# Attention with hashed masks, then a gated feed-forward: reordered turns, a later weight conversion and fewer transfers by ScalarE

## The chip, the cores and the metric

The kernel runs on one core of a Trainium2 chip. The time is that of the device, from start to end of the program, in microseconds (us); the median of 3 runs is 885.48 us (884.9 to 885.76). The profile is of one execution, with a span of 883.4 us from its first to its last instruction. The core's engines are TensorE (PE; its weight loads are the row PEld), VectorE (DVE), ScalarE (ACT), GpSimd (POOL) and SyncE (SP), which here only issues transfers (DMA).

## The reference

```python
batch, n_heads, seq, head_dim = (4, 8, 768, 64)          # q, k, v; proj is 64 x 6
q_bucket, k_bucket = ...    # 6 bits each: the signs of q @ proj and k @ proj
mask = q_bucket[:, :, :, None] == k_bucket[:, :, None, :]
scores = np.where(mask, np.matmul(q, k.transpose(0, 1, 3, 2)) / 8, -1e9)
attn = softmax(scores)                                     # over the keys, 1e-9 added to the sum
x = (attn @ v).transpose(0, 2, 1, 3).reshape(3072, 512)
h = x @ w_in                                               # 512 x 2048, given in float64
g = h * (1.0 / (1.0 + np.exp(-1.702 * h)))
return (g @ w_out).astype(np.float32)                      # 2048 x 512, given in float64
```

## The kernel before

Attention goes through 16 pairs of heads, n = 0 to 15, each in two halves of the queries, c = 0 and 1. (Pair 0 is cut finer, into four groups.) A group's body is given below. The instructions of TensorE, VectorE, ScalarE and GpSimd run in the order in which the code has them; those of SyncE are ordered by a scheduler. The scores come transposed (keys on the partitions): a product of small integer "feature" rows (`kf`, `qf`, from the hash bits) brings the mask into the same bank, and one exponential per tile of 128 keys unloads it.

```python
def featured(n):                        # hash bits -> feature rows, spread by 8 small transfers
    nc.vector.tensor_scalar(f, dots.pop(n), above[:, 0:1], weight[:, 0:1], ...)          # L413
    for c in range(2):
        for i, x in enumerate("kq"):
            queue = nc.scalar if (n, x) == (1, "q") else nc.sync
            for j in range(2):
                queue.dma_start(out=feats[n % 2][x][...], in_=f[...])                    # L420

def scores(n, c, kts):
    for kt in kts:
        ps = sps.tile(...)                                # three of these
        ... 2 products kf x qf and 2 products kT x qT into ps                            # L432
        nc.scalar.activation(es[c][:, kt, :, 0:HS], ps[...], Act.Exp, ...)               # L433

def values(n, c, kts):
    if 0 in kts:
        avs[n, c] = aps.tile([P, HS + 1], F32, tag="av", name="av")                      # one bank
    ... 12 products of v and e into av                                                   # L456

def unload(n, c): ...                   # ScalarE: av -> xT                              # L467, L468
def total(n): ...                       # TensorE: the sums of the exponentials, dn, in the one bank "m"
def invert(n):
    nc.vector.transpose(rt, accs.pop(n))                                                 # L484
    nc.vector.reciprocal(r, ...)        # 5 of them                                      # L486, L490
    nc.vector.transpose(rs, r)                                                           # L492

def begin(n):
    if n - 1 < len(in_chunks) - LATE:                     # 14 chunks of w_in, pairs 1 to 14
        conv[n] = convert(cv, *in_chunks[n - 1], nc.sync if n > 1 else nc.scalar)
        step(n)                                           # the load

for g in range(len(groups) + 2):                          # one group per half of a pair
    scores(n, c, kts)
    add_low(n, c)                       # GpSimd: acc0 = sum of the lower three e          L440, L441
    if hashes: featured(hashes.pop())
    add_high(*prev[:2])                 # VectorE: acc = sum of the upper three and acc0   L446, L448
    for x in turned:                    # "kq" in the first half of a pair
        turn(n + 1, x)                  # VectorE: kT, qT of the next pair                 L391
        measure(n + 1, x)               # ScalarE: their largest size                      L398
    while norms: norm(norms.pop(0))     # VectorE: xT *= rs                                L497
    if totals and totals[0][0] == g:
        norms.append(totals.pop(0)[1])
        total(norms[-1])
        invert(norms[-1])
    values(*prev)
    unload(*prev[:2])
    if "q" in turned: hashed(n + 1)     # TensorE, into "m"; then fetch q, k of pair n + 2
    step(n, 3)                          # three steps of the conversion
    if c == 0 and n > last - len(x_sums): x_sums[n - last - 1]()   # VectorE, pairs 12 to 15
    if c == 1: begin(n + 1)
    if g == len(groups) - 1: guard(0)   # VectorE: largest of all sizes
    if g == len(groups):
        guard(1)                        # TensorE turns it into "m" (row), VectorE reduces
        ...                             # GpSimd: sums of the first weights (s_in)
        next(ff)                        # the feed-forward begins
```

The conversion of a chunk of `w_in` from float64 is six operations of VectorE (L178, L182, L186 in the first half of a pair, L193, L195, L198 in the second) and one of ScalarE (L190, a square, issued with L186).

The feed-forward does both its products with seven instead of eight block products (Strassen-Winograd), twice nested in the second. Its last part, for the output, goes by steps `o` of seven products each; `after(0)` to `after(3)` are called within a step, between its unloading operations:

```python
def turned(c, i, j, q0, q1):            # VectorE: quarters of a block transposed into y[j]  L791
def written(sb, j, halves, queues):
    for b in halves:
        for a in range(4):
            queues[a % len(queues)].dma_start(out=dst, in_=ys[j][...])                   # L799

def after(at):
    if at == 0:
        while pending: pending.pop(0)()
    ...                                 # VectorE: sums of the next step's operands (t1, b12, t2, t4)
    if final and at == 2:
        for q in (0, 1, 3): turned(m, 1, 0, q, q + 1)
        written(sb, 0, (1,), loader + [nc.scalar])
    if final and at == 3:
        turned(m, 1, 0, 2, 3)
        written(sb, 0, (0,), loader + [nc.scalar])
...
elif o in (2, 3):
    pending.append(lambda a=ms[o], j=int(o == 3): turned(a, 0, j, 0, 4))
    if o == 3:
        pending.append(lambda sb=sb: written(sb, 1, (0, 1), loader))
```

Of the kernel before, what the change touches and what calls it, by code (L numbers as in the profile page):

```python
# [8 lines left out]
F32 = mybir.dt.float32  # L9
# [10 lines left out]
P = 128  # L20
# [18 lines left out]
def kernel(  # L39
# [17 lines left out]
    nc = tc.nc  # L57

    loader = [nc.sync]
# [223 lines left out]
    def attention(ff):  # L283
# [4 lines left out]
        with actx:  # L288
# [122 lines left out]
            def featured(n):  # L411
                f = wk.tile([P, HS], BF16, tag="f", name="f", bufs=1)
                nc.vector.tensor_scalar(f, dots.pop(n), above[:, 0:1], weight[:, 0:1], op0=Alu.is_gt, op1=Alu.mult)  # L413
                for c in range(2):
                    for i, x in enumerate("kq"):

                        queue = nc.scalar if (n, x) == (1, "q") else nc.sync
                        for j in range(2):
                            r0 = D * i + 32 * c + 2 * NB * j
                            queue.dma_start(out=feats[n % 2][x][D * j : D * j + 2 * NB, c * HS : (c + 1) * HS],  # L420
                                            in_=f[r0 : r0 + 2 * NB, :])
# [27 lines left out]

            def values(n, c, kts):  # L450
                if 0 in kts:
                    avs[n, c] = aps.tile([P, HS + 1], F32, tag="av", name="av")
                av, vt = avs[n, c], vts[n]
                for t in kts:
                    for j in range(2):
                        nc.tensor.matmul(av[D * j : D * (j + 1), :], vt[:, t, j, :], es[c][:, t, j, :],  # L456
                                         start=(t == 0), stop=(t == T - 1))
# [21 lines left out]
            def invert(n):  # L479


                dn = accs.pop(n)
                rt = st.tile([P, HS // 32, 32], F32, tag="rt", name="rt", bufs=1)
                nc.vector.transpose(rt.rearrange("p s i -> p (s i)"), dn)  # L484
                r = st.tile([P, 2, HS // 32], F32, tag="r", name="r")
                nc.vector.reciprocal(r, rt[:, :, 0].unsqueeze(1).to_broadcast([P, 2, HS // 32]))  # L486
                for r0 in range(0, P, 32):
                    c = r0 // 32 % 2
                    r1 = r0 + 32 - 64 * c
                    nc.vector.reciprocal(r[r1 : r1 + 32, c], rt[r0 : r0 + 32, :, 0])  # L490
                rs = accs[n] = st.tile([P, S], F32, tag="rs", name="rs", bufs=1)
                nc.vector.transpose(rs.rearrange("p (s i) -> p s i", i=32),  # L492
                                    r.rearrange("p c s -> p (c s)").unsqueeze(2).to_broadcast([P, S // 32, 32]))
# [13 lines left out]
                    next(conv.get(n, iter(())), None)  # L507

            def begin(n):
                if n - 1 < len(in_chunks) - LATE:  # L510

                    conv[n] = convert(cv, *in_chunks[n - 1], nc.sync if n > 1 else nc.scalar)
                    step(n)


# [16 lines left out]
            for g in range(len(groups) + 2):  # L532
                n, c, kts = groups[g] if g < len(groups) else (last + 1, 0, ())
                prev = groups[g - 1] if 1 <= g <= len(groups) else None
                if kts:
                    scores(n, c, kts)
                    if g == 0:
                        rest()
                    if kts[0] == 0:
                        add_low(n, c)  # L540


                if hashes:
                    featured(hashes.pop())
                ended = prev and prev[2][-1] == T - 1
                if ended:
                    add_high(*prev[:2])
                    if prev[1] == 1:
                        totals.append((g + (g == len(groups)), prev[0]))

                turned = ("", "k", "q", "")[g] if n == 0 else "kq" if c == 0 and n < last else ""
                for x in turned:
                    turn(n + 1, x)
                    measure(n + 1, x)
                while norms:
                    norm(norms.pop(0))
                if totals and totals[0][0] == g:
                    norms.append(totals.pop(0)[1])
                    total(norms[-1])
                    invert(norms[-1])  # L560
                if prev:
                    values(*prev)
                if ended:
                    unload(*prev[:2])
                if "q" in turned:
                    hashed(n + 1)
                    if n:
# [102 lines left out]
    def feed_forward(tag, late=()):  # L670
# [9 lines left out]
        with ExitStack() as fctx:  # L680
# [110 lines left out]
                    nc.vector.transpose(y, c[:, q].rearrange("p (b t) -> p b t", t=32))  # L791

            def written(sb, j, halves, queues):
                for b in halves:
                    blocks = slice(b * (TH // 32), (b + 1) * (TH // 32))
                    for a in range(4):
                        t0 = (2 * sb + j) * XT + b * TH
                        dst = out[t0 : t0 + TH, a * P : (a + 1) * P].rearrange("(b t) d -> t b d", t=32)
                        queues[a % len(queues)].dma_start(out=dst, in_=ys[j][32 * a : 32 * (a + 1), blocks, :])  # L799

            def product_of_halves(n, acc, after):

# [98 lines left out]
            for n, (sb, o) in enumerate(steps_out):  # L901
# [11 lines left out]
                def after(at):  # L913
# [15 lines left out]
                if o == 3:  # L929
# [6 lines left out]
                if o == 5:  # L936
# [13 lines left out]
    def whole(steps):  # L950
        for _ in steps:
            pass
# [46 lines left out]
```

## Time and profile before

| what | number |
|---|---|
| median time | 885.48 us |
| span of the profile | 883.4 us |
| TensorE clock granted, mean | 0.997 |
| score products L432, exponentials L433 | 155.1 us and 150.9 us busy |
| value products L456 | 131.8 us busy |
| bytes moved by DMA | 132.01 MB, mean 149 GB/s |

The page gives for each engine the time in which it was busy. Such a time says little by itself where several engines are nearly full; it has to be held against the waits, which name for every engine the instruction that it waited for, and the chain of waits, which follows the end of the program back to what released each step. A row of a transfer on SyncE or ScalarE is the time of its issue. Line numbers such as L432 are those of the kernel before.

### The profile page before, as it was taken

The page shows a single profiled execution, that of the slowest core. Times are in us where ns is not written, and L with a number is a line of the kernel's source. Part 1 is how long each engine was busy: PE and PEld are TensorE (multiplying, and loading weights), DVE is VectorE, ACT ScalarE, POOL GpSimd, SP SyncE. Part 2 cuts the span into 40 slices and gives each one's busy share as a digit, 9 for nine tenths or more (in the row PEclk, how much of TensorE's full clock was granted, in tenths as well). Part 3 has the DMA queues.
Part 4 walks back from the last instruction along what each step waited for, and adds up shares of the span by engine and source line. Part 5 has one row for each costly group of instructions (what it writes and reads, how often), then busy time and mean ns, then how long its engine had stood idle before and what let it go on. Part 6 is the DMA issues. An engine that isn't in the chain of part 4 may idle for free.

```text
span 883.4 us, 11926 instructions
## 1 busy us (share of the span) xinstructions
PE 866.9 (98%) x4077; PEld 498.4 (56%) x4077; DVE 724.9 (82%) x1020; ACT 313.3 (35%) x519; POOL 319.9 (36%) x275
## 2 busy tenths in 40 slices
PE   9899999999999999999999999999999999999995
PEld 5344444444444444444444444444888888888884
DVE  4599999999999956777777887888898977897785
ACT  5666677667667732223232223322000000000000
POOL 4244334333433363775433444559932000000000
PEclk9999999999999999999999999999999999999998
DMA  4755454566544103555456545575844665467524
GB/s 103 115 90 83 84 104 81 94 101 102 85 83 83 46 1 131 201 195 190 164 193 212 200 166 200 185 253 172 306 142 186 210 220 200 165 207 239 191 96 99
DMA packets 169477, 132.01 MB, mean 149 GB/s; under 512 B 123936, under 2 KB 138432, under 8 KB 164032
## 3 DMA queue, kind: packets, MB, share of 16 engines
q1 hardware_dynamic: 167712, 129.69, 51.7%
q10 hardware_dynamic: 1696, 1.48, 0.6%
q8 instruction: 34, 0.56, 0.3%
q14 instruction: 35, 0.29, 0.1%
HBM read 79.69 MB, written 50.33 MB: 147 GB/s over the span
## 4 chain that ended last, share of the span: by engine, by line
PE 96%; DVE 1%; DMA 1%; ACTq 0%; issue 0%; POOL 0%; ACT 0%; SPq 0%; POOLq 0%; DVEq 0%
PE product L699 33%; PE product L812 28%; PE ps L432 17%; PE av L456 14%; PE dn L477 1%; PE hash L408 1%; DMA q<-in_q_dram 1%; PE tp L366 1%; ACTq L420 0%; DVE xT L816 0%; PE hash L373 0%; DVE y L791 0%; SPq L328 0%; DMA qf<-f 0%; DVE rs L492 0%
## 5 line engine op out<-in xcount | busy, mean ns | idle before, releaser
L433 ACT ACTIVATE e<-ps 128x768 f32<-128x768 f32 x192 | 150.9, 811 | 18.4 <-PE ps L432 12.4
L432 PE MATMUL ps<-qT,kT 64*128 64x384 f32 x768 | 155.1, 482 | 0.0
L699 PE MATMUL product<-xT,w_in_sb 128*128 128x512 f32 x288 | 135.4, 592 | 0.0
L456 PE MATMUL av<-e,v 128*64 128x385 f32 x768 | 131.8, 490 | 0.9 <-ACT xT L468 0.9
L440 POOL TENSOR_TENSOR acc<-e 128x768 f32<-128x768 f32 x32 | 58.6, 1832 | 193.3 <-DVE acc L448 166.3
L707 ACT ACTIVATE c<-c 128x512 f32<-128x512 f32 x72 | 45.3, 630 | 186.3 <-issue 78.6
L456 PEld LDWEIGHTS av<-e,v 128*64 128x64 f32 x768 | 52.1, 136 | 77.6 <-issue 76.1
L699 PEld LDWEIGHTS product<-xT,w_in_sb 128*128 128x128 f32 x288 | 54.6, 190 | 68.5 <-issue 63.3
L699 PE MATMUL product<-t_x,s_in 128*128 128x512 f32 x192 | 90.2, 592 | 0.0
L432 PEld LDWEIGHTS ps<-qT,kT 64*128 64x128 f32 x768 | 68.2, 188 | 34.9 <-issue 34.8
L219 POOL TENSOR_TENSOR v<-c,u 128x512 f32<-128x512 f32 x24 | 34.1, 1423 | 127.7 <-ACT c L707 127.7
L818 ACT COPY u<-product 128x256 f32<-128x256 f32 x21 | 7.8, 372 | 167.7 <-PE product L812 125.5
L432 PE MATMUL ps<-qf,kf 64*128 64x384 bf16 x384 | 63.1, 324 | 2.9 <-ACT e L433 2.8
L699 PEld LDWEIGHTS product<-t_x,s_in 128*128 128x128 f32 x192 | 36.5, 190 | 45.9 <-issue 43.8
L441 POOL TENSOR_TENSOR acc<-acc,e 128x768 f32<-128x768 f32 x32 | 59.0, 1845 | 2.5
L699 PE MATMUL product<-xT,s_in 128*128 128x512 f32 x96 | 45.1, 592 | 0.0
L699 PE MATMUL product<-t_x,w_in_sb 128*128 128x512 f32 x96 | 45.1, 592 | 0.0
L432 PEld LDWEIGHTS <-kf 64*128 64x128 bf16 x384 | 19.1, 94 | 44.9 <-issue 23.4
L446 DVE SCALAR_TENSOR_TENSOR acc<-e 128x768 f32<-128x768 f32 x32 | 30.5, 954 | 7.7 <-ACT e L433 7.7
L467 ACT COPY vs<-av 128x1 f32<-128x1 f32 x32 | 5.1, 159 | 87.2 <-PE av L456 87.2
L812 PE MATMUL product<-raw_g,xT 128*128 128x256 f32 x152 | 35.1, 379 | 0.0
L448 DVE TENSOR_TENSOR acc<-acc,e 128x768 f32<-128x768 f32 x32 | 32.0, 999 | 3.3
(207 smaller groups left out, 1544.3 us busy)
## 6 DMA issues: line engine op xcount, KB each, us to landing
raw_g<-g_dram SPq DMA_DIRECT2D x22, 1024.0 KB
s_in<-g_dram SPq DMA_DIRECT2D x20, 1024.0 KB
g_dram<-c SPq DMA_DIRECT2D x72, 256.0 KB
g_dram<-t SPq DMA_DIRECT2D x48, 256.0 KB
raw<-in_moe_w_out_dram SPq DMA_DIRECT2D x16, 512.0 KB
raw<-in_moe_w_in_dram SPq DMA_DIRECT2D x15, 512.0 KB
v<-in_v_dram SPq DMA_DIRECT2D x32, 192.0 KB
g_dram<-u SPq DMA_DIRECT2D x24, 256.0 KB
```

The source lines that it names most:

```text
L219: return [lambda: eng.tensor_tensor(t1, b12, b11, op=Alu.subtract), lambda: eng.tensor_tensor(b12, b22, b12, op=Alu.subtract), lambda: eng ...
L366: nc.tensor.matmul(tp[D * j : D * (j + 1), i * P : (i + 1) * P], x[name][:, j, c * GT + i, :], ident, start=True, stop=True)
L432: nc.tensor.matmul(ps[:, j, 0:HS], a[hs, keys], m[hs, cols], start=not last, stop=last)
L433: nc.scalar.activation(es[c][:, kt, :, 0:HS], ps[:, :, 0:HS], Act.Exp, scale=1.0 / D**0.5)
L440: nc.gpsimd.tensor_tensor(acc, es[c][:, 0, :, 0:HS], es[c][:, 1, :, 0:HS], op=Alu.add)
L441: nc.gpsimd.tensor_tensor(acc, acc, es[c][:, 2, :, 0:HS], op=Alu.add)
L446: nc.vector.scalar_tensor_tensor(acc, e[0], T * TINY, e[1], op0=Alu.add, op1=Alu.add)
L448: nc.vector.tensor_tensor(acc, acc, x, op=Alu.add)
L456: nc.tensor.matmul(av[D * j : D * (j + 1), :], vt[:, t, j, :], es[c][:, t, j, :], start=(t == 0), stop=(t == T - 1))
L699: nc.tensor.matmul(ps, wq[LEFT[i]][:, kc, :], xq[RIGHT[i]][:, kc, :], start=(kc == 0), stop=(kc == K2 - 1))
L707: nc.scalar.activation(c, c, Act.Gelu_apprx_sigmoid)
L812: nc.tensor.matmul(ps, wq[LEFT[i]][:, c, :], gq[RIGHT[i]][:, c, :], start=(c == 0), stop=(c == F4 - 1))
```

## The change

It has six parts: pair 1's feature rows for the queries are issued by ScalarE for one half of the queries only; a chunk of `w_in` is converted one pair later, and its first load is issued by SyncE; the sums are turned (the first operation of `invert`) between the turn of the keys and that of the queries; the last values take the bank "m", so as not to wait for the unloading of the ones before, and the guard's two parts come two groups earlier; the keys of pair 2 are fetched a group earlier in the code; and at the end the last two products are turned back quarter by quarter within their steps, and the output is written by fewer transfers on two queues.

```diff
-                        queue = nc.scalar if (n, x) == (1, "q") else nc.sync
+                        queue = nc.scalar if (n, x, c) == (1, "q", 0) else nc.sync
...
-                    avs[n, c] = aps.tile([P, HS + 1], F32, tag="av", name="av")
+                    pool, tag = (mps, "m") if (n, c) == (last, 1) else (aps, "av")
+                    avs[n, c] = pool.tile([P, HS + 1], F32, tag=tag, name="av")
...
-                nc.vector.transpose(rt.rearrange("p s i -> p (s i)"), dn)
+                nc.vector.transpose(rt.rearrange("p s i -> p (s i)"), accs.pop(n))
+                yield
...
-                if n - 1 < len(in_chunks) - LATE:
-                    conv[n] = convert(cv, *in_chunks[n - 1], nc.sync if n > 1 else nc.scalar)
+                if 0 <= n - 2 < len(in_chunks) - LATE:
+                    conv[n] = convert(cv, *in_chunks[n - 2])
                     step(n)
...
-                for x in turned:
+                inverted = iter(())
+                for x in turned[:1]:
                     turn(n + 1, x)
                     measure(n + 1, x)
...
                     total(norms[-1])
-                    invert(norms[-1])
+                    inverted = invert(norms[-1])
+                    next(inverted)
+                for x in turned[1:]:
+                    turn(n + 1, x)
+                    measure(n + 1, x)
+                whole(inverted)
...
-                    for x in "kq":
+                    for x in "kq" if n else "q":
                         if n + 2 <= last:
                             fetch(n + 2, x)
                     fetch_v(n + 1)
+                elif turned:
+                    fetch(n + 2, turned)
...
-                if g == len(groups) - 1:
-                    guard(0)
+                if g in (len(groups) - 3, len(groups) - 2):
+                    guard(g - len(groups) + 3)
                 if g == len(groups):
-                    guard(1)
...
             def written(sb, j, halves, queues):
-                for b in halves:
-                    blocks = slice(b * (TH // 32), (b + 1) * (TH // 32))
-                    for a in range(4):
-                        ...
-                        queues[a % len(queues)].dma_start(out=dst, in_=ys[j][32 * a : 32 * (a + 1), blocks, :])
+                first, last = halves[0] * TH, (halves[-1] + 1) * TH
+                for a in range(4):
+                    ...
+                    queues[a % len(queues)].dma_start(out=dst, in_=ys[j][32 * a : 32 * (a + 1), first // 32 : last // 32, :])
...
-                    if final and at == 2:
-                        for q in (0, 1, 3):
-                            turned(m, 1, 0, q, q + 1)
-                        written(sb, 0, (1,), loader + [nc.scalar])
-                    if final and at == 3:
-                        turned(m, 1, 0, 2, 3)
-                        written(sb, 0, (0,), loader + [nc.scalar])
+                    if n + 2 >= len(steps_out):
+                        for q in ((0,), (), (1, 3), (2,))[at]:
+                            turned(m, int(final), int(not final), q, q + 1)
+                    if final and at >= 2:
+                        written(sb, 0, (3 - at,), loader + [nc.scalar])
+                    if n + 2 == len(steps_out) and at == 3:
+                        written(sb, 1, (0, 1), loader + [nc.scalar])
...
-                elif o in (2, 3):
+                elif o in (2, 3) and n + 2 < len(steps_out):
```

More of the change, by code (lines that the diff above doesn't have):

```diff
@@ L479, in invert @@
             def invert(n):
-                dn = accs.pop(n)
                 rt = st.tile([P, HS // 32, 32], F32, tag="rt", name="rt", bufs=1)
-                nc.vector.transpose(rt.rearrange("p s i -> p (s i)"), dn)
+                nc.vector.transpose(rt.rearrange("p s i -> p (s i)"), accs.pop(n))
+                yield
                 r = st.tile([P, 2, HS // 32], F32, tag="r", name="r")
@@ L793, in written @@
             def written(sb, j, halves, queues):
-                for b in halves:
-                    blocks = slice(b * (TH // 32), (b + 1) * (TH // 32))
-                    for a in range(4):
-                        t0 = (2 * sb + j) * XT + b * TH
-                        dst = out[t0 : t0 + TH, a * P : (a + 1) * P].rearrange("(b t) d -> t b d", t=32)
-                        queues[a % len(queues)].dma_start(out=dst, in_=ys[j][32 * a : 32 * (a + 1), blocks, :])
+                first, last = halves[0] * TH, (halves[-1] + 1) * TH
+                for a in range(4):
+                    t0 = (2 * sb + j) * XT
+                    dst = out[t0 + first : t0 + last, a * P : (a + 1) * P].rearrange("(b t) d -> t b d", t=32)
+                    queues[a % len(queues)].dma_start(out=dst, in_=ys[j][32 * a : 32 * (a + 1), first // 32 : last // 32, :])
             def product_of_halves(n, acc, after):
```

## The prediction

> **What bounds the kernel now.** I read the page's first part, then the busy time by stretches, then every wait of TensorE, then the chain of waits for the first 60 us and for the end.
>
> ```profile
> PE 866.9 (98%) x4077; PEld 498.4 (56%) x4077; DVE 724.9 (82%) x1020; ACT 313.3 (35%) x519; POOL 319.9 (36%) x275
> ```
>
> TensorE is busy for 866.9 of 883.4 us, and the change removes none of its products. Everything that can be won is therefore in the 16.5 us without a matmul. Where these lie (the columns are the stretch, its length, then busy time and count of PE, PEld, DVE, ACT, POOL, then clock, DMA share and GB/s):
>
> ```profile
> 10.00:23.00 13.00, 12.86 (x82) 5.80 (x80) 6.35 (x8) 8.92 (x13) 4.85 (x4) 1.00 0.37 59
> 23.00:43.00 20.00, 17.06 (x124) 7.59 (x124) 10.96 (x20) 12.42 (x20) 4.82 (x3) 1.00 0.71 116
> ...
> 60.00:320.00 260.00, 260.00 (x1808) 117.79 (x1802) 242.43 (x307) 176.07 (x277) 98.00 (x54) 1.00 0.49 83
> 320.00:345.00 25.00, 24.13 (x92) 10.07 (x89) 12.45 (x19) 6.71 (x12) 13.49 (x13) 1.00 0.14 50
> ...
> 869.00:884.00 15.00, 4.11 (x20) 3.27 (x18) 4.96 (x12) 0.00 (x0) 0.00 (x0) 0.78 0.62 139
> ```
>
> About 3 us are missing between 23 and 43, 0.9 near 323, and some 10 at the end, after the last product. Between 60 and 320 nothing is missing: no change of order can win there, but VectorE, busy for 242.4 of these 260 us, can lose. The waits of TensorE (total, times, longest) name the releasers:
>
> ```profile
> PE ps L432 <- ACT e L433: 2.8, 2, 1.6
> ...
> PE av L456 <- ACT xT L468: 0.9, 1, 0.9
> ```
>
> And the chain of waits (start, us, what) tells why the exponentials of L433 were late twice:
>
> ```profile
> 24.87 1.58 ACTq L420
> ...
> 26.48 0.74 ACTq L420
> ...
> 27.25 0.72 ACTq L420
> ...
> 31.08 5.27 DMA q<-in_q_dram
> ...
> 36.37 0.98 DVE qT L391
> ...
> 41.45 0.02 ACT raw L190
> ...
> 42.02 0.80 ACT e L433
> ...
> 54.45 1.42 PE dn L477 x8
> ```
>
> First ScalarE issues four small transfers and a large one from 24.87 to 29.31, and its next exponential starts only at 28.78; TensorE stands from 28.65 to 29.84, 1.19 us. Then pair 2's q lands at 36.36, VectorE turns it, turns the sums, inverts, and converts; ScalarE's square (L190) stands in its in-order queue behind that conversion, and the exponential behind the square starts at 42.02: TensorE stands 1.61 us. At 54.45 the sums' product takes 1.42 us where elsewhere it takes 0.78, since VectorE is still late with `acc`: 0.64 us more, hidden in a "busy" row. At the end:
>
> ```profile
> 872.30 1.54 DVE L791 STREAM_TRANSPOSE y<-xT 128x256 f32<-128x256 f32 x3
> 873.70 0.40 DVE L816 TENSOR_TENSOR xT<-product,xT 128x256 f32<-128x256 f32 x1
> 874.13 0.63 DVE L791 STREAM_TRANSPOSE y<-xT 128x256 f32<-128x256 f32 x1
> 874.19 2.66 ACTq L799 DMA_DIRECT2D out_dram<-y  x4
> ```
>
> The last block is turned at 874.76, yet the span ends at 883.4. SyncE's own waits hold 3.7 us for earlier transfers of `out`; its last four issues start at 873.87, 877.16, 877.58 and 879.58, and data move until about 881.4.
>
> **What the Trainium skill says.** "Perfetto Trace Analysis", section "Identifying the Most-Contended Engine", warns that matmul busy time is no measure of the distance to the roofline. The trace agrees: the 1.42 us of `dn` are counted as busy. Its section "DMA Instruction — HWDGE (DVE, Sync)" says that a row of a transfer on an issuing engine is descriptor generation and not the movement. The trace agrees: the row of the last issue ends at 880.04, while data move until 881.4. "DMA: Bandwidth & Descriptors", section "Issuing engines are not separate DMA queues", says that a second issuing engine saves only sequencer time. The trace agrees that this time is not small for ScalarE: 1.58, 0.74, 0.72 us each. "SBUF — State Buffer", section "Who interferes with whom", says that a two-input VectorE operation contends with a GpSimd operation's reads; here the same conversion step takes 0.69 us alone and 2.03 us at 301.62, beside GpSimd's `acc`.
>
> **The change part by part.**
>
> *Transfers by ScalarE.* Of its four feature transfers two go to SyncE, and the conversion's load goes to SyncE as well, where in the new instruction order it stands ahead of pair 1's keys. ScalarE is free at 24.87+1.58+0.74+gaps = 27.3 instead of 28.8. The first exponential then ends at 28.1, before TensorE gets there (28.65), and each following one (0.80) keeps pace with its score product (0.81). Gain 1.19. The load (512 KB, some 2.5 us at the 200 GB/s seen here) moves to about 4 to 8 us; DMA is 10 to 22% busy between 6 and 8 us, and pair 1's keys are turned at 14.58 without a wait on a transfer, so I take no loss there.
>
> *Conversion a pair later.* In pair 1, L178, L182 and L186 (0.65+0.69+0.69) and the square go, and q's four transfers no longer share the DMA with that load. The exponential waits for nothing but its scores. Gain 1.61. The second half of that conversion (1.98+2.05+0.69 at 47.12 to 51.98) also goes from between pair 1's two sums, so `acc` is ready long before `dn`. Gain 0.64. In return pair 15 gets a conversion. There VectorE runs some 5 us later than now between 316 and 327, and so GpSimd's sums of the weights about 2 us later; the product that needs them starts 15 us after the last scores begin, and by the same addition the third sum is ready after 13.4. So I take nothing, with about 1.2 us in hand.
>
> *Sums turned between keys and queries.* Now VectorE does kT (0.97), qT (0.94), then rt (0.58) once `dn` is there; in later pairs it idles for `dn`:
>
> ```profile
> 231.75 0.58 DVE L484 STREAM_TRANSPOSE rt<-dn 128x384 f32<-128x384 f32 x1 [0.60 <-PE dn L477]
> ```
>
> In the new order qT no longer fills that time: idle before rt becomes 0.60+0.94 = 1.54, and all that follows, `acc` of the next sums included, comes 0.94 later. In an ordinary pair this is free (`acc` ends at 229.37, its second use by TensorE is at about 231.3). In pairs 12 to 15 one operation of 1.22 us (x_sums) is added, the loop of VectorE grows to 19.95 us against TensorE's 19.53, and it falls behind by 0.42 each time. Already now `dn` takes 0.97 at 289.5 and 1.19 at 309.2, or 0.6 us too much together. Starting 0.94 later I get excesses of 0.2, 0.4 and 0.7 at three `dn`s (the last with the 0.18 of the reduction that moves ahead of it), 1.3 in all. Loss 0.7.
>
> *The last values in another bank.* The last `av` no longer waits for the unloading of the one before. The bank it takes instead is free once VectorE has reduced `row`, by my sum near 317, and the values start at 323. Gain 0.87. The turning of `largest` (0.27) moves only.
>
> *Quarters and fewer writes at the end.* In the last but one product three of four transposes move from after it to inside it: its own VectorE chain runs up to 1.6 us later, t2a is ready at 865.6 and needed at 866.04, so it just fits. In the last product the first quarter is turned early: the stretch at 872.30 has two transposes instead of three, about 0.5 us less, so the first half can be issued at 873.3 and the last quarter is turned at 874.25. Sixteen transfers of 128 KB become four of 256 and eight of 128, half on each queue. In the program's order each transfer uses one of eight completion counters in turn; the last eight then wait only for writes that are long done, where now SyncE's wait for ScalarE's of a moment before. After 873.3 plus 0.8 us to the first byte, 1.05 MB at 233 GB/s (what 1.05 MB took from 868.7 to 873.2) end at 878.6; with the 2.0 us from the last byte to the end, 880.6 or so. Against 883.4: gain 2.7.
>
> Sum: 1.19 + 1.61 + 0.64 + 0.87 + 2.7 - 0.7 = 6.3 us, from 885.48 to **879.2 us**.
>
> **The rivals.** (a) Pair 2's feature rows become the new wait. SyncE issues keys, queries, values and these rows one after the other, up to 48.85 now, just when TensorE starts pair 2 (49.43). With TensorE 2.8 us earlier, the first four rows must land by 46.6; SyncE can start only 1.3 us earlier, as ScalarE's measuring of the keys gates it, and I get about 45.7. For it: SyncE is solidly occupied from 36.6 to 48.9. Against: later halves are needed later, and the large load is gone. It would give back up to 1.5 us: 880.5. (b) VectorE becomes the bound throughout: if the 0.94 us don't fit, each of the fifteen pairs loses some tenths, and the time would be 882 to 885. Against: the loop is 18.93 us of 19.53. (c) The end is bound by the rate of the DMA or by completion and not by issue: then the end wins 1 us instead of 2.7, 881. For it: the DMA share is near full while 1 MB moves. (d) The late sums of the weights or t2a stop TensorE: each up to 1 us. (e) The end wins more than I think, if two queues reach 280 GB/s as in single slices: 878.
>
> **Range and chances.** The rivals (a), (c) and (d) each cost 1 to 1.7 us with perhaps one chance in four; (e) and a smaller loss of VectorE win about 1 each. So 877.0 to 881.6. Faster by over 2% would need 17.7 us, more than TensorE's whole idle time: 1%. Slower by over 2% would need a collapse of the steady pairs: 1.5%.
>
> **What would show it.** Right: no wait of `ps` for `e` between 23 and 43; `dn` of 0.78 at pair 2; no wait of `av` near 320; conversions from pair 2 to pair 15; idle before rt grown to about 1.5 us; `dn` above 0.78 in the last three pairs, 1.3 us too much together; no wait of SyncE for `out` at the end, and the last issue near 875.5. Wrong: a wait of TensorE for `kf` or `qf` near 46, for `s_in` near 325, gaps in every pair, or an end still 8 us after the last transpose.

## Result and the profile after

| | before | after |
|---|---|---|
| median time | 885.19 us (884.59 to 886.24, 6 runs) | 882.06 us (881.22 to 883.58, 6 runs) |
| ratio | | 0.9965, 95% interval 0.9952 to 0.9977 |
| span of the profile | 883.4 us | 880.0 us |
| first product of the feed-forward starts | 328.45 us | 324.36 us |
| TensorE's last product ends | 873.11 us | 869.33 us |
| last quarter turned, after that | 1.64 us | 2.04 us |
| end of the span, after TensorE's last product | 10.26 us | 10.69 us |

The kernel is 3.1 us faster; 6.3 were predicted. The last four rows (read from the two traces) divide it: 4.1 us won before the feed-forward, 0.3 lost in it, 0.4 lost behind TensorE's last product, where 2.7 had been expected. So the middle of the prediction held and its end failed. Line numbers are now those of the changed kernel, up to 10 higher.

First the page's first part, then the busy time by stretches, in the same columns and the same four stretches as before.

```profile
PE 866.7 (98%) x4077; PEld 497.6 (57%) x4077; DVE 725.3 (82%) x1020; ACT 314.5 (36%) x519; POOL 321.8 (37%) x275
```

```profile
10.00:23.00 13.00, 12.86 (x82) 5.79 (x80) 6.33 (x8) 8.92 (x13) 4.88 (x4) 1.00 0.41 65
23.00:43.00 20.00, 20.00 (x146) 9.10 (x146) 12.71 (x21) 15.27 (x23) 6.07 (x4) 1.00 0.55 96
...
60.00:320.00 260.00, 260.00 (x1797) 117.35 (x1795) 241.73 (x307) 174.54 (x273) 98.91 (x54) 1.00 0.46 83
320.00:345.00 25.00, 25.00 (x82) 10.68 (x79) 17.79 (x23) 6.45 (x11) 17.71 (x17) 1.00 0.26 89
```

TensorE's busy time is what it was. Its holes between 23 and 43 us (2.94) and between 320 and 345 (0.87) are full. The waits of TensorE no longer hold `ps` for `e` or `av` for `xT`; besides a wait at the start, these are left:

```profile
PE product L820 <- ACT xT L830: 0.6, 1, 0.6
PE product L820 <- ACT t_x L830: 0.4, 1, 0.4
```

The chain of waits, which had led through ScalarE's issues, q's transfer, VectorE and ScalarE, now runs through TensorE alone:

```profile
28.63 4.95 PE ps L432 x36
...
37.24 4.95 PE ps L432 x36
...
51.17 0.78 PE dn L479 x8
51.96 4.03 PE av L458 x24
```

The value products of pair 1's second half start at 51.96 instead of 55.87. The price of turning the sums first is in the same view, between 260 and 310 us:

```profile
266.06 1.23 PE dn L479 x8
...
286.04 1.22 PE dn L479 x8
...
306.01 1.32 PE dn L479 x8
```

Unhindered `dn` is 0.78. Here 0.45, 0.44 and 0.54 are lost, 1.43 together; before it was 0, 0.19 and 0.41, the last two being these:

```profile
289.51 0.97 PE dn L477 x8
...
309.23 1.19 PE dn L477 x8
```

And the end, in the timeline:

```profile
869.37 1.08 DVE L800 STREAM_TRANSPOSE y<-xT 128x256 f32<-128x256 f32 x2
...
870.48 3.63 SPq L807 DMA_DIRECT2D out_dram<-y  x4
870.49 3.41 ACTq L807 DMA_DIRECT2D out_dram<-y  x4
870.74 0.63 DVE L800 STREAM_TRANSPOSE y<-xT 128x256 f32<-128x256 f32 x1
```

All went as the change intended: two transposes in place of three before the first half can go, eight writes on two queues. SyncE's waits of 3.7 us for `out` are gone, and the last issue ends 2.74 us after the last transpose, where it had been 5.28. Yet the last byte comes 6.34 us after that transpose (before: 6.63) and the end 8.65 (before: 8.61). Issues that end 2.5 us sooner moved the end by nothing. Most of the data does come sooner: 95% of the last block's packets have ended 4.99 us after the last transpose, before 6.34. In the kernel before, the DMA is nearly idle for about 1 us (a share of 0.10, the last but one number) while an issue of 1.96 us holds up the last one:

```profile
879.00:880.00 1.00, 0.00 (x0) 0.00 (x0) 0.00 (x0) 0.00 (x0) 0.00 (x0) 0.50 0.10 20
```

This hole is gone. But the last 5% of the packets take another 1.36 us (before: 0.28), and from the last byte to the end it is 2.31 us (before: 1.98). That is the question for the experiments.

A lead is what TensorE does after its last product. This is the line of the closing branch (the fallback for large inputs, not entered here), seen by engine, with min/median/max in ns, of the changed kernel:

```profile
L971 PEldq COMPARE_BRANCH  x2: 83/1982/3882, 866.5 to 869.5; - x2
L971 DVEq COMPARE_BRANCH  x2: 51/53/55, 871.4 to 871.6; - x2
```

```profile
L1004 DVEq DRAIN  x2: 10/34/58, 874.7 to 879.6; - x2
```

```profile
L962 PEldq COMPARE_BRANCH  x2: 92/1742/3393, 870.0 to 873.3; - x2
```

TensorE's branch takes 3.88 us where VectorE's takes 0.05; in the kernel before (the last view) it took 3.39. The short row of VectorE deceives: its next instruction (the DRAIN of L1004, in the second view) starts at 874.74, 3.17 us after its second branch, and ScalarE's at 878.58, 3.23 us after its own. So at all three over 3 us pass there, with TensorE within the row and with the others behind it. In the trace two packets of 16 KB on the DMA queue for instructions follow TensorE's last product, one of them from 870.51 to 871.96, within that branch and just when the eight writes are issued, and the two slow issues among these (1.56 on SyncE, 1.20 on ScalarE) end 0.4 us after it. In the kernel before, two slow issues among the last eight (1.23 and 1.96) end 0.48 and 0.44 us after such packets.

### The profile page after: what moved, and what is told of

Read it like the earlier page. It is cut to its first block, busy times and chain, and to the rows that moved or that the text cites. A ratio compares the mean times of both kernels' runs of the same rounds, so it can differ in the third digit from the quotient of the medians.

```text
span 880.0 us, 11896 instructions
## 1 busy us (share of the span) xinstructions
PE 866.7 (98%) x4077; PEld 497.6 (57%) x4077; DVE 725.3 (82%) x1020; ACT 314.5 (36%) x519; POOL 321.8 (37%) x275
## 4 chain that ended last, share of the span: by engine, by line
PE 95%; DVE 3%; DMA 1%; issue 0%; ACT 0%; SPq 0%; ACTq 0%; DVEq 0%
PE product L708 33%; PE product L820 26%; PE ps L432 18%; PE av L458 15%; PE dn L479 2%; PE hash L408 1%; DVE xT L824 1%; DVE y L800 1%; DMA q<-in_q_dram 1%; PE hash L373 0%; PE tp L366 0%; DVE v L824 0%; DVE t4g L222 0%; DVE s_in L220 0%; DVE xT L948 0%
```

## The experiments

Two theories for the end. A: the fetch of instructions at the closing branch holds up the issue and the packets of the last writes, whatever their layout. B: the layout counts (queues, sizes, who issues), and something in the new one gives back what it gains. For attention the rival readings were those of the prediction. For comparing starts I use the time from the first score product to the first product of the feed-forward: 317.88 us before, 313.82 after. The first score product itself comes between 9.9 and 11.4 us, and so the span of a single profile is uncertain by 0.7 us. Counted from there, eight profiles with the changed attention give 313.8 to 314.3 us; a difference of a few tenths says nothing.

**The new end alone**, in the kernel before (the last three pieces of the printed diff, and no others).

```diff
+                first, last = halves[0] * TH, (halves[-1] + 1) * TH
...
+                    if final and at >= 2:
+                        written(sb, 0, (3 - at,), loader + [nc.scalar])
+                    if n + 2 == len(steps_out) and at == 3:
+                        written(sb, 1, (0, 1), loader + [nc.scalar])
```

> The kernel before with only the new end (last two products turned back by quarters, four transfers of 256 KB and eight of 128 KB on two queues). Theory A (the new end gains nothing: ScalarE issues the writes of the first block ahead of its own copy of u, so VectorE runs late in the last product, and the last megabyte then moves no sooner): from the end of the last matmul to the end of the span about 10.6 us as after, against 10.3 before; time within 0.5 us of before, 884.7 to 885.7. Theory B (my prediction's sum: the end gains 2.7 us by itself, and something else ate it in the full change): time about 882.5.

885.72 us, ratio 1.0009 (1.0000 to 1.0017). From TensorE's end to the span's end 10.80 us, where before had 10.26. The new end alone wins nothing.

**The rest without it**: the changed kernel with the old end, the reverse of that diff.

> The changed kernel with the end of the kernel before. Theory A: keeps all of the gain, 4 us of attention less 0.2 to 0.4 us on the way: 881.3 to 882, so no slower than the full change. Theory B: 2.7 us slower than the full change, 884.8.

881.76 us, ratio 0.9964 (0.9951 to 0.9976), the same as the whole change. So all that the change wins is won in attention.

**Block 1 by SyncE alone.** In the changed kernel ScalarE issues two of the four large writes of the last block but one, and these wait for VectorE's transpose.

```diff
-                        written(sb, 1, (0, 1), loader + [nc.scalar])
+                        written(sb, 1, (0, 1), loader)
```

> The changed kernel, the four writes of block 1 issued by SyncE alone. Theory A: ScalarE's copy of u no longer stands behind them; the idle time of 1.49 us of VectorE before its first addition of the last product goes, the last transpose ends about 0.7 us sooner after the last matmul (1.3 us instead of 2.04), and the span shrinks by 0.7 us, if SyncE's four issues are done before the last block's. Rival (VectorE is late by its four more transposes alone): the last transpose stays 2.0 us after the last matmul.

881.91 us, ratio 0.9967 (0.9954 to 0.9979). The last transpose ends 1.31 us after TensorE instead of 2.04. The reason stands in the timeline of the changed kernel:

```profile
863.34 0.91 ACTq L807 DMA_DIRECT2D out_dram<-y  x2
...
864.34 0.37 ACT L826 COPY u<-product 128x256 f32<-128x256 f32 x1 [13.59 <-PE product L820]
...
864.74 0.42 DVE L824 TENSOR_TENSOR xT<-product,u 128x256 f32<-128x256 f32 x1 [1.49 <-ACT u L826]
```

ScalarE's copy of `u` stands in its in-order queue behind two issues that wait for VectorE, and VectorE then idles 1.49 us for the copy. This explains why the last quarter is turned 0.4 later and not 0.5 sooner. What mending it wins isn't settled: in this profile the end follows TensorE by 9.62 us instead of 10.69, in three later kernels with the same edit by 10.3 to 10.4, and the median, 0.15 us lower, can't tell.

**No fallback.** The changed kernel without the closing read of the flag and the branch (it leaves out the fallback).

```diff
-    unsafe = nc.values_load(largest[0:1, 0:1].bitcast(I32)) >= SAFE_BITS
-    loader[0] = nc.scalar
-    with tc.If(unsafe, preferred_fallthrough_block=False):
-        ...
```

> The changed kernel without its last part: the test of the largest size and the conditional fallback behind it (not entered with these inputs) are left out, so no engine jumps over code at the end and no instructions of it are fetched. Theory F (instruction fetches of 16 and 8 KB take DMA engines while the last megabyte is written; they hold up two issues for 1.2 to 1.6 us and leave stragglers): the issues after the last matmul all take under 0.6 us, the last one ends by 1.5 us after the last transpose instead of 2.74, the last byte comes at most 5.2 us after it instead of 6.34; the span shrinks by 1.5 us or more (the closing branch itself, some 0.5 us, goes as well). Theory R (the rate at which 1 MB of 512-byte rows moves sets the end): the last byte still comes 6 us after the last transpose, and the span shrinks only by the closing branch, under 0.7 us.

879.85 us, ratio 0.9943 (0.9927 to 0.996), 2.2 below the median of the changed kernel, 1.9 by the ratios. From the last transpose to the last byte 4.85 us instead of 6.34, to the end 6.32 instead of 8.65. The last block moves at 232 GB/s between its 5% and its 95%, against 201 with the branch. Of the 2.3 us, 1.5 lie before the last byte and 0.8 behind it. Behind it, with the branch, SyncE goes through its waits for the eight completions twice, once before the branch (to 878.43) and once behind it (878.69 to 879.14). One expectation failed: the issues were to take under 0.6 us and end by 1.5; without any 16 KB packet the last ones still take up to 1.20, and end 2.24 us after the last transpose.

**Half of the last bytes.** The changed kernel, with half the columns of the last block left unwritten (0.52 MB less).

```diff
-                for a in range(4):
+                for a in range(2 if len(halves) == 1 else 4):
```

> The changed kernel, which writes only half of the last block's columns: four transfers of 128 KB after the last matmul instead of eight (half of that block is left unwritten, 0.52 MB). Theory R: at some 200 GB/s the last byte comes 2.6 us sooner after the last transpose, 3.7 instead of 6.34, and the time falls by 2 to 2.6 us. Theory F: the two slow issues stay, and the last byte comes only as much sooner as the stragglers allow: about 5 us, time down 1.3 us or less. Theory C (a fixed delay of completion and closing dominates): under 0.7 us.

879.62 us, ratio 0.9944 (0.9927 to 0.996). The last byte comes 3.04 us after the last transpose, 3.3 sooner, but from there to the end it is now 3.1 instead of 2.3. There the end no longer hangs on the data: SyncE is through with its waits at 876.44, but ScalarE's next instruction after its branch starts only at 877.06, 3.67 us after it, and the end follows at 877.88. The run halves the last issues along with the bytes, so it doesn't tell the two apart.

**The old end without the fallback**: the kernel before with the same cut.

> The kernel before without its closing read of the flag and the conditional fallback behind it. Theory A: the fetch of instructions at that branch holds up the last writes in both kernels, so without it the old end too becomes some 2 us shorter: from the end of TensorE's work to the end of the span 10.3 becomes about 8.3, the time about 882.6, ratio 0.997, and the new end (8.38 with the same cut) is then still no better than the old one. Theory B: without the fetch the number of writes shows: the old end with its sixteen writes stays at 9 or more, time 884 or more, and the new end would have gained 0.7 or more if nothing had been fetched there.

883.02 us, ratio 0.9977 (0.997 to 0.9984), 1.9 below the kernel before. From TensorE's end to the span's end 7.62 us. These are the last issues of that kernel and of the changed one without the fallback, from the timelines:

```profile
874.91 0.63 DVE L791 STREAM_TRANSPOSE y<-xT 128x256 f32<-128x256 f32 x1
874.98 1.98 ACTq L799 DMA_DIRECT2D out_dram<-y  x4
```

```profile
871.04 3.05 SPq L807 DMA_DIRECT2D out_dram<-y  x4
871.05 3.13 ACTq L807 DMA_DIRECT2D out_dram<-y  x4
871.30 0.63 DVE L800 STREAM_TRANSPOSE y<-xT 128x256 f32<-128x256 f32 x1
```

ScalarE's four issues before, which took 2.66 us with the branch, take 1.98. Without the branch the old end comes 5.99 us after its last transpose and the new one 6.32; the last byte 4.77 and 4.85, at 224 and 232 GB/s. Both layouts feed the DMA fast enough. That the old one stays 0.76 ahead counted from TensorE's end is its earlier transpose (0.43) and 0.25 between last byte and end. Of A and B, A fits: the branch with the fallback behind it costs both kernels about 2 us, and without it the new layout still wins nothing. That it costs them by fetching instructions is argued, not shown.

**A short block behind the branch** (it leaves out the second attention and feed-forward and keeps four sums of weights by GpSimd), and **the flag only**, read and not used (it leaves out the fallback).

```diff
     with tc.If(unsafe, preferred_fallthrough_block=False):
-        with tc.tile_pool(name="cv3", bufs=1) as cv:
-            ...
-        whole(feed_forward("2"))
+        for f in in_sums(0):
+            f()
```

> The kernel after with its closing branch kept, but with a short block behind it (it leaves out the fallback, the second attention and feed-forward, and keeps four sums of weights by GpSimd). Theory A (the distance of the jump counts, since the instructions behind it must be fetched): TensorE's branch takes well under 1 us and not 3.9, no issue of the last eight takes over 1.2, from the end of TensorE's work to the end of the span 8.4 and not 10.7, time 879.9. Theory B (the branch itself, with the barrier around it, counts): the branch stays near 3.9 us, the span's end at 10.7, time 882.

> The kernel after with the flag still read by every engine but with no branch and no fallback behind it. If reading the flag costs nothing, as both theories have it, the end is that of the kernel with neither: 8.4 us from TensorE's end, time 879.9. If the reading is what holds the end, 10.7 and 882.

880.37 us, ratio 0.9947 (0.993 to 0.9963), and 880.12 us, ratio 0.9941 (0.9925 to 0.9958). Reading the flag costs nothing: 6.38 us from the last transpose to the end, as without it. With the short block TensorE's branch takes 0.18 us:

```profile
L970 PEldq COMPARE_BRANCH  x2: 87/134/180, 862.0 to 862.2; - x2
```

and no 16 KB packet follows it. But the branch now stands 7 us before TensorE's end, not behind it, and the last transpose comes at 2.88, so this run doesn't keep the place apart from the distance. VectorE and ScalarE go on 0.20 and 0.16 us after their branches. The medians lie 1.7 and 1.9 us below that of the changed kernel. Shown is that it is the branch with the full fallback behind it, and not the flag; that the distance of the jump counts, and not the place, is likely but only argued.

**The parts of attention, one back at a time**, each in the changed kernel, one profile each: all four feature transfers of pair 1's queries by ScalarE; the conversion a pair earlier; the last values in their old bank.

```diff
-                        queue = nc.scalar if (n, x, c) == (1, "q", 0) else nc.sync
+                        queue = nc.scalar if (n, x) == (1, "q") else nc.sync
```

```diff
-                if 0 <= n - 2 < len(in_chunks) - LATE:
-                    conv[n] = convert(cv, *in_chunks[n - 2])
+                if n - 1 < len(in_chunks) - LATE:
+                    conv[n] = convert(cv, *in_chunks[n - 1])
```

```diff
-                    pool, tag = (mps, "m") if (n, c) == (last, 1) else (aps, "av")
+                    pool, tag = (aps, "av")
```

> The changed kernel, pair 1's four feature transfers of the queries all issued by ScalarE again. Theory: ScalarE is free at about 28.7 instead of 27.3 and TensorE stands before the first score products of pair 1 for 1.2 to 1.4 us again (their start at 29.8 to 30.0 instead of 28.63). Rival (the large load on ScalarE's queue was the cause): no wait.

> The changed kernel with the conversion a pair earlier again (pairs 1 to 14), its first load still issued by SyncE at the start and the sums still turned between keys and queries. Theory (the conversion in pair 1 stood before the exponential by way of ScalarE's square, and made VectorE late for pair 2's sums): the load is there early and q lands earlier than before the change, so most of the 1.9 us does not return (0 to 0.8 us), but dn of pair 1's sums takes over 1.0 us. Rival (a pair later is what removed the wait): 1.6 to 1.9 us return at the second half of pair 1. At the other end, pair 15 without a conversion changes nothing at the start of the feed-forward (within 0.2 us).

> The changed kernel with the last values in the bank of the others again. Theory: TensorE waits 0.9 us for the unloading between the last two groups of values (around 320 us), as before the change, and the feed-forward starts 0.9 us later counted from the last score products. Rival (the wait is hidden now by VectorE's lateness): under 0.3 us.

From the first score product to the feed-forward 315.07, 315.71 and 314.92 us, so 1.25, 1.89 and 1.10 above the 313.82 of the whole change (times of the single runs 882.46, 883.0 and 882.21 us). With the first the old wait of `ps` for `e`, 1.2 us, comes back, with the second one of 1.0 and a `dn` 0.6 longer, with the third the wait of `av`, 0.9. The second didn't go as expected: nearly all of the 1.9 us returned and not 0 to 0.8, so it is the later pair that removed the wait, as the rival had it. The three add up to 4.24; the whole stretch had won 4.06, the order of the sums having cost some of it. The earlier fetch of pair 2's keys, to which the prediction gives no term, was not put back alone.

**The sums turned last**, behind keys and queries, as before, in the changed kernel; then the same with block 1 by SyncE; then also with the four sums of the first products' operands in pairs 9, 11, 13 and 15 instead of 12 to 15.

```diff
-                for x in turned[:1]:
+                for x in turned:
...
-                for x in turned[1:]:
-                    turn(n + 1, x)
-                    measure(n + 1, x)
...
-                    if c == 0 and n > last - len(x_sums):
-                        x_sums[n - last - 1]()
+                    if c == 0 and n in (last - 6, last - 4, last - 2, last):
+                        x_sums[(n - last) // 2 - 1]()
```

> The changed kernel with the sums turned after both keys and queries, as before. Theory: the three long sums' products (1.23, 1.22 and 1.32 us at pairs 13 to 15) fall to about 0.8, 1.0 and 1.2, so the attention part ends about 0.7 us sooner; no wait comes back in pair 1, because the conversion is gone from there, or at most a few tenths since VectorE turns the sums only after q has landed. Rival (the order is needed in pair 1): TensorE waits again for the exponential or the hash between 23 and 43 us, by 0.5 us or more.

> The changed kernel with the sums turned last again and block 1 written by SyncE alone. Theory: the two gains add, 0.7 us in the attention and 0.7 to 1.0 us at the end: 1.4 to 1.7 us under the changed kernel, 0.9947 of before. Rival (the end is held by the last bytes and the fetches whatever comes before): only 0.7 us, 0.9957.

> The kernel h1 with the four operations on x (1.22 us each) in pairs 9, 11, 13 and 15 instead of 12 to 15. Theory: VectorE's loop of some 18.9 us exceeds TensorE's 19.5 by 0.6 us in such a pair and wins 0.6 us back in the next, so no sums' product is longer than 0.9 us; the attention ends another 0.7 us sooner, 0.994 of before. Rival (the lateness is from elsewhere, for example operations beside GpSimd's): the long ones stay.

The changed kernel ran once more beside the last two:

> The changed kernel again, beside the two that follow on the same chip: 0.9965 of before, within 0.001.

Sums last: 881.66 us, ratio 0.9963 (0.9949 to 0.9977). The three late `dn` fall from 1.23, 1.22, 1.32 to 0.78, 0.96, 1.30: 0.7 us, of which 0.4 reach the feed-forward (the first scores of pair 2 take 0.3 longer here). With block 1 by SyncE 881.3 (ratio 0.9948, 0.9935 to 0.9961), with the sums spread 881.37 (0.9955, 0.9943 to 0.9967), against 882.33 (0.9963, 0.995 to 0.9976) for the changed kernel again. Spread, every `dn` takes 0.78: VectorE's loop is what was too full. But these two kernels scatter: 880.25 to 882.66 and 879.58 to 883.29. The profile of the first, its slowest run, shows one reason, in its chain of waits:

```profile
31.62 5.02 DMA q<-in_q_dram
...
36.66 0.98 DVE qT L391
37.64 0.48 DVE rt L485
...
38.16 0.85 PE hash L408 x8
```

When pair 2's q lands late, qT stands ahead of the turned sums on VectorE, TensorE waits 1.5 us for the bank that `rt` frees. In the order of the change `rt` stands ahead of qT and needn't wait for q: a guard for one pair, paid for in three others. That the guard works is argued and not shown. No profile of that order met a late q; the changed kernel's own six runs lie between 881.22 and 883.58, and with the sums last alone five lie between 880.83 and 881.85.

**The order kept in pair 1 alone**, sums last elsewhere, the sums spread, block 1 by SyncE.

```diff
-                for x in turned[:1]:
+                cut = 1 if n == 1 else len(turned)
+                for x in turned[:cut]:
...
-                for x in turned[1:]:
+                for x in turned[cut:]:
```

> The kernel after with the sums turned between keys and queries in pair 1 alone and behind both elsewhere, the sums formed in pairs 9, 11, 13 and 15, and block 1 of the last writes by SyncE alone. Theory A (the order guards pair 1 against late queries and costs VectorE 0.7 us in pairs 13 to 15): the sums of the denominators take 0.85 each there, the stretch from the first pair to the second is 17.6 and not 18 to 19, the feed-forward begins 312.6 or less after the first product of the first pair (after: 313.8), time 880.5, ratio 0.995. Theory B (the order does nothing for pair 1, the long stretches of the two earlier kernels are late loads that nothing mends): the stretch is 18 or more again, time 881.5, ratio 0.996.

880.11 us (879.75 to 880.47), ratio 0.9949 (0.9935 to 0.9962). No `dn` above 0.78, no wait of TensorE between 20 and 345 us, 312.68 us from the first scores to the feed-forward, and the scatter is down to 0.7 us in five runs. This version lies below both kernels: 4.8 us below the kernel before (884.91 beside it) and, by medians that were not taken side by side, 1.95 below the changed one; by the ratios to before, whose intervals overlap, 1.4. Not all was as expected: from pair 1's first `dn` to its second it takes 17.88 us and not 17.6, since the first scores of pair 2, at 45.81, take 5.24 instead of 4.95. Their second product with `qf` starts 0.31 us after the first, where both start together in the changed kernel, which points to the late feature rows of rival (a); the trace names no wait. As q wasn't late in this profile, the guard wasn't put to the test in it.

## Why the prediction was right or wrong

- **Where TensorE's idle time lies: right.** The holes named were the ones filled. But that between 60 and 320 us "no change of order can win" is not so: by its own count 0.6 us of late `dn` hide there in busy time, and with the sums spread every `dn` takes 0.78.
- **Transfers by ScalarE, +1.19: right.** Put back, it costs 1.25, with the same wait of 1.2.
- **Conversion a pair later, +1.61 and +0.64: right in mechanism.** At pair 1's second values 3.91 us are won with the transfers' share, where 3.44 was the sum. By the starts of the groups in both traces the two stalls were 1.26 and 1.79 where the waits named were 1.19 and 1.61, and 0.2 more was won ahead of pair 2's hash. "dn" at pair 2 is 0.78, as said.
- **Last values in another bank, +0.87: right**, 1.10 by itself.
- **Sums' order, -0.7: right.** The three late `dn` lose 1.43 instead of 0.6, so -0.83 against -0.7. The excesses came out as 0.45, 0.44, 0.54 and not as 0.2, 0.4, 0.7; the loop of 19.95 us is met, with 19.97 from 286.04 to 306.01. Idle time before `rt` was to become 1.54 us and is 0.74 (at 227.84), since `kT` now starts only 1.72 us ahead of `rt` where it was 2.43: VectorE's whole loop runs later against TensorE. Rival (b), a loss in every pair, didn't come.
- Together attention was to win 3.61 us and won 4.1 at the feed-forward's start. Some 0.3 went in the feed-forward, where the wait for ScalarE's `xT` is 0.6 and had been 0.4.
- **The step that failed is "Quarters and fewer writes at the end", gain 2.7; the end lost 0.4.** It took the old end to be bound by issue, SyncE's 3.7 us of waits and its late last four issues, and so every issue won was a gain. Of its terms: *"the last quarter is turned at 874.25"*, 1.14 us after TensorE, took 2.04, as ScalarE's writes hold up its copy of `u` (shown by giving them to SyncE: 1.31). *"1.05 MB at 233 GB/s end at 878.6"*, 4.35 after that turn, took 6.34 with the branch and 4.85 without. *"The 2.0 us from the last byte to the end"* were 2.3 with the branch and 1.5 without. What it left out is the branch behind TensorE's last product, which the profile before shows as 3.39 us on TensorE's sequencer, in the rows not counted as busy. Its own sign of being wrong came, an end still 8 us after the last transpose: 8.65.
- What the runs showed in its place: beside the branch, the earlier issues do bring 95% of the last block 1.35 us sooner, but the last packets trail, so that the last byte comes only 0.3 sooner, and the later turn and the longer way from last byte to end take that back. Without the branch there is nothing to win: last byte 4.77 us after the last transpose with the old writes, 4.85 with the new ones. Why the last packets trail beside the branch stays open. That the time from last turn to end, put at 6.35, measures 6.32 without the branch is luck in part: its two terms are off by +0.5 and -0.5.
- **Rival (c)**, an end bound by rate and completion, came nearest, but it still granted 1 us. Without the branch, old and new ends move the same bytes at 224 and 232 GB/s. With it, the old end did lose about 1 us to a late issue (the hole at 879 us), so the reading of the waits was not all wrong; what was won there was lost again behind it.
- **Rival (a)**, the feature rows of pair 2, only touched: in the repeat of the changed kernel a wait of 0.2 us for `qf`, with the stretch to the feed-forward 0.5 longer, and with the sums last the same scores take 0.2 to 0.3 longer. In the changed kernel's first profile there is none of it, so it is not what was lost. Rivals (d) and (e) didn't come: no wait of TensorE for `s_in` or `t2a`, and no rate of 280 GB/s over the last block.
- One reading of the trace was wrong: the conversion step of 2.03 us beside GpSimd's `acc` doesn't take 0.69 "alone". Its rows of 0.69 (L193, from 356 us on) also stand beside GpSimd's operations, but have one input in another memory (PSUM, where TensorE's products go). Steps with both inputs in SBUF and no GpSimd operation beside them, such as L182 in attention, do take 0.69. Nothing in the sum rests on it.

The Trainium skill, "DMA: Bandwidth & Descriptors", section "Issuing engines are not separate DMA queues", which the prediction cited for ScalarE in attention, says that a second issuing engine saves only sequencer time. These runs agree for the end: both kernels have ScalarE issue four of the last eight writes, and in the changed one the last issue ends 2.5 us sooner after the last transpose while the end comes at the same distance.

## What to carry to other kernels

An engine's wait for its own earlier transfers is not yet a gain to be had: before counting an earlier issue as one, compute the bytes still to be moved over the rate, and look at what else moves then, rows not counted as busy included. A transfer that a compute engine issues holds up that engine's next work if it has to wait for its data: here ScalarE's copy, and with it VectorE for 1.49 us. And an order meant to guard one early stage against a late load belongs in that stage alone: kept everywhere, it takes slack from the stages where the engine has none.

## What the runs showed of the hardware

- A closing branch over the whole fallback, which isn't entered, costs some 2 us at the end of this program (medians 882.06 to 879.85, and 884.91 to 883.02). TensorE's branch takes 3.88 us; VectorE's and ScalarE's rows take 0.05, but their next instructions start 3.17 and 3.23 us later. With a short block behind the branch, which then stands elsewhere, these are 0.20 and 0.16. 16 KB packets of instructions travel among the last writes. In the two kernels compared, the four slow issues beside them take 1.2 to 1.96 us; without the branch the issues of the last block take 0.3 to 1.2.
- The first scores begin anywhere from 9.9 to 11.4 us, in kernels with the same beginning. A profile against a profile can't tell tenths of a us unless one counts from there, and even then the same attention gave 313.8 to 314.3 us.
- Writes of 256 KB moved no faster than those of 128 KB by SyncE: the last block but one at 191 GB/s on two queues and 194 by SyncE alone, against 226 before.
